# Turning q and k by transpositions of two row halves in place of quarter products, in an attention and bilinear FFN kernel

## The chip, the cores and the metric

The kernel runs on one core of a Trainium2 chip. The metric is the device time of one execution in microseconds (us). The core has five engines that run side by side, each through its own list of instructions in order: PE (TensorE, matmuls; its weight loads are shown apart as PEld), DVE (VectorE), ACT (ScalarE), POOL (GpSimd) and SP (SyncE). SP and ACT issue the DMA transfers here, and 16 DMA engines carry them out. A matmul takes its two operands from SBUF, the memory on the core, and writes to PSUM, a small memory[...] from which DVE and ACT take the results.

## The reference

```python
batch, n_heads, seq, head_dim = (8, 12, 448, 64)
n_tokens, d_model, d_ff = (3584, 768, 1536)

def rmsnorm(x, g):
    rms = np.sqrt(np.mean(x * x, axis=-1, keepdims=True) + 1e-06)
    return x / rms * g
q_n, k_n = (rmsnorm(q, g_q), rmsnorm(k, g_k))
scores = 1.0 / np.sqrt(q.shape[-1]) * np.matmul(q_n, k_n.transpose(0, 1, 3, 2))
scores = scores - np.max(scores, axis=-1, keepdims=True)
attn = np.exp(scores)
attn = attn / (np.sum(attn, axis=-1, keepdims=True) + 1e-09)
attn_out = np.matmul(attn, v)
x = attn_out.transpose(0, 2, 1, 3).reshape(B * S, H * D)
return (x @ w_a) * (x @ w_b) @ w_out
```

Inputs and output are fp32; the three weight matrices come in fp64. q and k are normalized per row of 64, attention runs over 448 positions in each of 96 heads, and its output goes through a bilinear feed-forward layer.

## The kernel before

**Attention** runs in 24 steps p, each of four heads of one batch: two pairs w = 0, 1 of two heads. For each p one tile each of q, k and v is loaded (function `loads`, line L424): pair w lies in partitions 64 w to 64 w + 63, its two heads h side by side, and each partition holds 7 consecutive positions j of 64 values. So a tile is [128, 2, 7 x 64], and a DMA moves runs of 7 x 64 values (1,792 bytes). Tiles of q and k have one buffer each, those of v two.

In `normalize`, ACT squares a tile (L459), DVE adds up the squares (L461) and scales them (L494), and POOL raises them to the power -0.5 (L496). DVE multiplies q by the result into the tile `qn` (`apply`, L500). k is not multiplied: its factor is applied later, as the scale of Exp.

A product of queries and keys needs both with head_dim on the partitions, so q and k are turned (`transposes`, and `turn_first` for p = 0). The turn is done on the PE by `quarter_turns` (L528): for each of the 7 positions j, 2 pairs w and 2 heads h a 64x64 block is multiplied with an identity, on one quarter of the PE's array. The result stands in a PSUM tile `pt` of two banks, one per pair, with head h in partitions 64 h to 64 h + 63. ACT copies it to `qkT` (L547 for k, L549 for q with the gains). The tile `pt` has the tag `sc`, of which there are two buffers, shared with the scores.

After that come, for each of the 7 blocks j of keys: `scores` (L587, four products on quarters of the array, tile `sc`), Exp of each head by ACT (L593, two of 448 columns), and `values` (L609, four products, accumulated in the tile `o`). The sums over the keys come from products with ones (L645) for p < 4, and for later p from additions by DVE and POOL (L623) and one such product. `invert`, `put_out` and `divide` do the division.

**The feed-forward layer** takes two batches at a time (beta = 0 to 3) and multiplies by a scheme with seven products in place of eight. Its first layer is `quarter_products` (L1294) for beta = 0 and 1 and `deep_products` (L871) for 2 and 3, its second `last_product` (L995) and `inner_products` (L1192). All of these are full-array products of 128x128. Before that, ACT and DVE round the fp64 weights to fp32 (`rounding`, L247 to L256) while attention runs.

**The order of the work** is not found on the chip. The kernel books 4,383 operations with `op(...)`, each with its engine, an expected duration, what it reads and writes and, on the PE, a mode ("quad" for quarters, "full"). `Plan.run` then issues them in a sequence that is written out in the source as the compressed string `ORDER`. Each engine's instructions follow in that sequence, and the semaphores between the engines follow from the tiles. The durations in the calls were for the making of the sequence and have no effect when the kernel runs; the same is so of the mode. In the sequence, feed-forward products of the two batches before stand among the attention of the next ones.

At the start the PE runs `warm` products (L409, identity by identity, 128x128) until q and k of p = 0 are there.

In the first part of the time, p = 0 to 11 lie within the first 220 us; p = 12 to 14 at 386 to 450; p = 15 at 536 and 686; p = 16 to 23 at 739 to 875. What follows is the feed-forward layer alone.

Of the kernel before, what the change touches and what calls it, by code (L numbers as in the profile page):

```python
# [20 lines left out]
def _float_of(bits):  # L21
# [11 lines left out]
    "c-rkZ2Xs}%wtHqyyXEwAOLEgg=m-g@5Aq_#hN2G<5JZZif$$(9KnP$U2@pU!5)cA01p)|sAPK!E7{Me)s#uT@ND+McY`n&=``iTZum4=@y|2Hy"  # L33
    "*mKXEGc&u--ZT3$;NDJ(B)<~~p~M5K=`sBlF%8QwJ&Mn75Tmn4(Xput{#M`vGPsvSx*;5#q2LIeGZ-8`-;DbupOp>M%x81qzU=!Z_j&ccrzW23"
    "o%!^H4F1FM<3<CpQPA)>j7%XT9!)003A|XHopU&6PIh+QKG^G>z8i|Iob^yx#;-1dRsS}rVDqGcjq3|GxK;rxgXP6gG@<BC@~=x_-0S0D<ziU4"
    "{AT{5?_klAuNM@3wE%usSayBE{8A_>D7kc%FaFFZeDhQ9mh)t_0c<0Da2C$2UwVqXUbdEOaFLR-l7Cr4ifjH-44sca^?|DI>foDi=Ix(nl3jam"
    "?A^s3-hJ&LckmKi^dEq{iv3XjF@fznpwd}+63WXfH^ZhaTjAJ&qwgHNCBUXX?5o-b^A5q@uMh0|66o3+aDDq4C@rsqedYV#-@E6+xo!1zjy)gl"
    "-u*%CnQc&W6pn8>+OVa%`t9nQf2=<Cef80AkG%8smbbsE+H$rU&RnZHbhzQ#p+oi1srLNlTItySqx(14?AvtYWbKh7M~=Q<Q(qHSf28hWT`hR4"
    "_gH(5Jw|HYQ9(I)u=*g}Jb2*1SKoXIJl%fd#*Wrdx$7_2ukPA)`R3)zyRLt8{mNILeOdY07nL_|^t^cS^U90zg)8b6$K?xRrEux|?<>!L`uV5-"
    "eC=w*l|NrSckS}!KV7+UIilj~Clw!8Uihfu{EqV#pMJXi%JvHnpR2fdQ9QrnA5WgEIPr1isk0w!ue^2ZM8oMn{rTh{w%<Ha(eQr5_h-Kge0#Ry"  # L40
    "Y~2~FzV7s?y1L5amrm4PxOm~z@$>K3Hq<t}_g=#XwYTa||GECX`ucO<D{=MTHhff9USD2U{YCld>t{bNFTeWsl@9@`o!d@B6&(8H5Y&8FbMQSl"
    "P+bevf2^v4jdh1>H^c8?KS1o>6R>CP?)R!b+g*8aUB%k-`?ssxw*hP``S_!XHL#7qX(u%7*?(&ftlkLgHk6gGU%zVWx~hYPhgQKBQea#Lcw_m6"
    "m6Yb^zX8ih{!;g8a{AN~fW?bo(ZU9}xo`n2m``BtTsS;8kJ8z&fIyzh1-X!$13B4{Jq@xkZ>GSc$uKE%3Z)qt851)o5E!>O9n!}Fq@_aY7}Equ"
    "NdXv1k_o`e!vS7;5ndby!-m4JAvp8G3or=gzc3I6z;kYQf9MN+pM_`p06fzhdXuN&siy!yc>*2>H$3_Xz{5SDM|bGn4Z0IE2>~E6DUm{FfL}cb"
    "F1WuFbm|C@5D)PkP;|R?0Bvb&)T(6*6c*PEn#DqF48%s`C^9lKB8rC7Fl7e>2>4y#^PUB-2f#AHGypUWKvxJMu3VBsa&t*;4#~;R70J|T(>^Mg"
    "YE6A(MoxCtG{_RN_{oze2?Q8G4uP?0S+8cLO-Y+FJ?*tzwq<rIOdcaLmILY2U}P%7*x9M6dG%?jspHa93Q{~PMvfdcYGewGn3J4L^I*)&Fltox"
    "@RXF{!$(XWo-%6kh?EJ*h59S$FTJ#amsNhKd+?BvjuFYj9E0HbLC?SV;-DczpMTzwJn*>z0|vSW3>`4Ak2`(9fd2gl_U|S1e^z+n8DV(O-aWbG"
    "XI~k@4etGd_>|yy`0<DPJ^q-Z$D_hCQV*e5k6zI2iJn~7BtGe(HNWou(9_+x#3#|Qi9Hh^c`Wha#2$&gdL(x1*`r(c?%iBnx+FdHxT|v#=X44a"
    "9i0VNCjo@`_zvwK?I=k-dI)X1wG{+LDaV>WNV)qdqaua&gfRQp5<A>ckf_}=8e(^N#DYD>ed3r#7?OlB8jA1lIm%f+i+Vkbr<y^Ty~a@lk(oSa"
    "w-~#Nj^;VPKa}J4dXa@`Qo~^O32!(2AcUhD$2b<wvC;rajEG>=@1@jY)Fg&MwY#{sT12(w1oiMUYU6=P3Frj0LD<=iLLYbr;}m!UM?G!aDC7&l"  # L50
    "MF7JjU>O8D8cH7mzflOdNYF;$h=#Zkl!n>(sD>@UN2wRZTS017Qwhk<TLjY$Nkk9?;Tt!6P2h_uaGhq1p`$0D2YyS>lhGqakN7Q1`JT`*<Ye;j"
    "FOyGQBQL#-3S5NxAxCS^4g2JsleC7>Ge;;_SM^R+)!WqrYwPG?I{4_<2Wkd$Uvf992kq&9Xb*R27q@Hg`Q1DF?b@-kA5_9Kr^-)OpP<M49NtIk"
    "f75$2J+^7nvF$*%l=u2-_n|}ouwiGf^_%we+I{J*b-gw~rSQah*jfgqXG+(Wo-Exh9zVWj{m#-gWu+x+N^6RXONwhY7H@^34eK`*?SE^-UMRb~"
    "yX?`OW##b5sxsJIu&H=spOuA$eF}HN>Ov?u_U`DS)msZ{3RbVKhQo)Kttwas-Ip(2R=O-df6dOK(vrf$!nOGu^9xs<E?!;s=BicsC8Y%=b?+9h"
    "Dk^w$>B_FKdIg?p%lGbuq-C&k>B7~O3o4c@TKVfYRxDb+Xny`ex^%<qOKHiH{KTd6<{ewSaOJAS3+Js^{>H)s%jPD|U(jXot_7WUyw-L8obq{d"
    "X3v|oY4)tQX63D)MZ3&Qnm(P)on5kE_N?5wujS?)nK^T2?vj~HXTH8@&#W0U9-Kj6%gvoVeO7MXrRlj{rsu9(H#0kX+JjSzvx|zdr?LmK9?Y4N"
    "4J12zDr7CqdOa&^e%8DPUY$rY=FHj(c?mNo&Bz>&2kF|0853awOu72nl=0&WCXS!karuO09rDx1rKe3!%bc8<nU*;*Eh8;+cEZG*jPa=%sjrTo"
    "Iwk$p^z_V~nVG4OHlchh)OAQ7dn|41eW{~IkA^9uMrEc<Ov%VdNg3a6!pL#y>21=-jvWhQ$0nyHk7+Y{%qzKVaz~HKgA~YXl`?YDh#9T&^0Km^"
    "<rEk)xaIg^T=vkhQ-?xa+?X*i8sZ>kL`+OS+V>?&BcdWG)<#bT!UO&K1^V_4*x?`I^Z6hNIG^Q#2f)Cy)HJ$ioi$KF*RZ1MAcLy3{*@b(LdUb9"
    "nIbvdnEbp0L=H0qgWf|_rFp=c-!WA6sNtHbs=DgaR1-hi8>*q{ieFI-MNvAas->7ZR%@zX^(&^Pw6k&THBB=*dKDAXNke3>VrZRo9TQUzlND?}"  # L60
    "T~^{%)uV*Vrly5xR;ZQW({wou=|WVb(pA}`D5$Wf6$&z}1j95m{E(5@E6cjtLDP`8tf@HEbWKk1$d;n38ZuE#S(S}=tRJ-iqWcYhN5hX(a=2{h"
    "x@`E25KWJ0uWP0eYG_`~w2&ALGXkot*!o+jnc6N4jZn~RMT^%BO*UmiR?!j}1r#N`soO3<MP-zWGitnQgv+uf%YIZYLDRfy1QLX!ma=ZBTAJBj"
    "vs6<LSK~ru%kSx6Aw3!t@|>as^>6Qy!(`1sa>Z0+*>fLSs-RmNt<~aDzN{-gT-5H@(Us^5v@TSZ1I<DVt%L6MYBp+!9ujIr#ap^J+|W(0ZiMQV"
    "H{OcWEkh6JvS!I43DG9{7I(>G?~-Dn!HU^d2}R?5%DZS4ZjDuqWq62fFB;KF_n--Aw;ZCN8&$>E0kJGpSCjo17E^G;g4Ts#tXQajJn?v>R}?N("
    "bUS?xhr{D=aHixY4zY!UxJ*&#>6WPIaEPMJ;+z9a!O2O2(p8WIL4HyYBquNPN;J`_lEj5LD04b3>T+<BqzHTq%9>F^qDfS=5J^ZB-f0oxB!u`w"
    "yM*|oqPhnB_lJZg_!-$2O51rn;T|s|9t)f4H$w@c`P=y;{H^_hpY!^(SkvPPL#0)sYnnyDtrH(+iq_nz>TNL!UCs#28Rjyn+X7zFCCMSlE?Fj`"
    "U`03umq0<_Ig#UecN?yah^ZuF0#PsofiMoW5^3;O!J93nE0rCL0p)uDCxTtB@OU*c#t3C`qC{g1kwo%*0^iIZNQ$u{!YLQvxCp|S8Ol6Hh++67"
    "W-^tvH<+x8n(TASZi}fd!4%sVZqX-+ZoK;)Oyw9a^1Q%{ju@uN9FyC*7?YV>ViIqEAdTc|CAplE$#8-<n9l4AT8ec@I&+Ik8<)#LWI?35&hyBN"
    "IyixgqfBBNM;UHJODCm*Q=*dSX96eiRN|;WWl5uI1l9>06PZhBj`u!Z&CHDj1K&yzC^F=621)U0E>WjwQ0f-jQqFBR(dFbFoXiO#dQ^;aa#Tm}"
    "7+7+Mbf+s0z3o6xQ{JW)*Kty?`d}QgccQVhxrlfQM{RMmmEaUCE(Z%C&DM-^ShqN1sROl8&>+z%Hh<Y|$CN7ZoSR4UILTI=j|?iWv=Af-T_P}r"  # L70
    "=WM-coC|FX%A;tl#8WYjLvwgWoj@d>cpYdi6EwTt(Fl&?IO1SL<cYz_|0GHx7biG4P2#Y35y{=0F(=dcV7;YMh4LRdV|nomZV+{&iyS0aLNPvq"
    "xQXO!ElIc|4nhP*%3T=#5+h8CV?5z0!*H~*UAU@aI$%JwcFIo9<>KVogjaYBFsJ?SM2hBAyVUASoMcQ;0Ean*tk6Zo)y&}>AS80=3(EE8I3hB%"
    "gD@BGjN~0rxcNlDMmZ!v&7929nh-IT#Kd4O60rqoLAYi#lqY@?8G(0@FU%Jm9TV{R0={;Bf7@{4ZAn_h+CyJxNQfug?+y4`hP7zv^Tq{2eV%A$"
    "SrJhdW@^{ahrA({-%nzQ5lbwO$BHll7N)Py^qS4Qa*Sq1StPod8SaZ#!wsVAG(sbIpqZvg67WQiG&Lhk4p+QB#bx<rx7)2_c*!nzdzahN+L$JW"
    "h&LK{F*efWjtY|lm`HxN<Wh;~6daP%3JDcx2v0E3+ek!`#OA8(h$9h>2pYu)Fs*pXxdf~YaqkpL1Jp?aj7k)1WgpK|V1~-cGWtEh5fAZ+R4^zq"
    "15g?8c8QCzi}{c7X7~8dg$B#=CLr*C3dql)82KCMf7<d7fWptk>2Kgk@4o5nKT`CL7(5K@QDYw**&PXXjc>5C(0<XT4$1!`#vPzR^ro)qMH?Bw"
    "9cE1ue!xCR+W1BPGt<8UK%21eA7LXd-0pARW=$;aeBHLqHkvkRd51}(B5+$fn@1D*9lR#5G&$|=CXw5NAa>If`{7oSzi&tX?!9O5{|@L+!nC89"
    "{xGKRqSD4i8bk=b8liD~mpC{TTxG%K#=&idO^CD+6Pg&@A%nX-o4DK-`2%r30&rKI+uFh%hPO3qvgfXG^hdlwf96mkKYw)o_)&c)Uw)h^x&8aA"
    "^S@Xi|LY9y!7l;mJs13VhLE2tr|u=&J@|zj67;__;r=UWL;mM(xqE4R4}K#2J5;O;O8"
# [68 lines left out]
def kernel(  # L148
# [126 lines left out]
    def fast_body(ld, wk, ps_s, ps_o, ps_mm, dram):  # L275
# [139 lines left out]
        def loads(p, nm):  # L415
# [4 lines left out]
            def emit():  # L420
                x = ld.tile([P, 2, NT * D], FP32, tag=nm, name=nm + "_sb", bufs=2 if nm == "v" else 1)
                for w in range(2):
                    pair = src[b, h0 + 2 * w:h0 + 2 * w + 2]
                    nc.sync.dma_start(x[low_high[w]], pair.rearrange("h (p j) d -> p h (j d)", j=NT))  # L424
                xs[nm, p] = x
            if p == 0 and nm != "v":
                def begin():
                    xs[nm, p] = ld.tile([P, 2, NT * D], FP32, tag=nm, name=nm + "_sb", bufs=1)

                def half(w):  # L430
                    pair = src[b, h0 + 2 * w:h0 + 2 * w + 2]
                    queue[("SP", "ACT")[w]].dma_start(
                        xs[nm, p][low_high[w]], pair.rearrange("h (p j) d -> p h (j d)", j=NT))
                op(None, 0.0, -11, begin, [], [f"{t}/{w}" for w in range(2)], new=[t])
                for w in range(2):
                    op(("SP", "ACT")[w], 0.7, -10, lambda w=w: half(w), [], [f"{t}/{w}"], kb=350)
                return
            op("SP", 1.28, p - (1.8 if nm == "v" else 2.0), emit, [f"firsts{PREP}"] if p >= HELD else [], [t], new=[t],
               kb={"q": 620, "k": 620, "v": 530}[nm], dmas=2)

        def loaded(p, nm):
            return [f"{nm}0/0", f"{nm}0/1"] if p == 0 else [f"{nm}{p}"]

        def normalize(p):
# [8 lines left out]
            def squares(s, nm):  # L453
                sq = tile_of(f"sq{nm}{p}", "sq", 1)

                def square():
                    x = xs[nm, p]
                    t = xs["sq", nm, p] = wk.tile([P, 2 * NT, D], FP32, tag="sq", name="sq")
                    nc.scalar.activation(t, x.rearrange("p h (j d) -> p (h j) d", d=D), AF.Square)  # L459
# [3 lines left out]
            def front(n):  # L463
# [10 lines left out]
                def times():  # L474
                    if n == 0:
                        qns[0] = wk.tile([P, 2, NT, D], FP32, tag="qn", name="qn")
                    nc.vector.tensor_tensor(
                        qns[0][:, :, j0:j1],
# [1094 lines left out]
```

## Time and profile before

| | |
|---|---|
| time, median of 3 runs | 1479.97 us (1479.83 to 1484.28) |
| time of the profiled execution | 1479.91 us |
| its span in the trace | 1478.1 us |
| PE busy | 1461.7 us, 99%, 10,238 matmuls |
| DVE, ACT, POOL busy | 986.4, 437.6, 328.9 us |
| DMA | 248.28 MB in 152,036 packets, mean 168 GB/s |
| granted PE clock | 0.999 |

A group line of the profile reads: source line, engine, operation, output<-input by tile names, tile of the array (for the PE), shape and count; then the sum of busy time and the mean ns of one; then the time that the engine stood idle before them and what ended it. A line of the timeline reads: start in us, length in us, engine, source line, operation, tiles, shape and count, and in brackets the idle time before. A matmul's length holds its way through the array, which overlaps with that of the next ones; what it occupies of the PE is the distance from its start to the next start. The first rows of the page divide the span into 40 equal slices and give busy tenths (9 is 90% or more). The chain of waits is followed back from the last instruction, at each step to what released it.

### The profile page before, as it was taken

To read this page: it belongs to the slowest core of one execution; us is meant where nothing else is said; L and a number is where in the kernel's file an instruction comes from. 1 tells how busy PE (TensorE), PEld (TensorE's weight loads), DVE (VectorE), ACT (ScalarE), POOL (GpSimd) and SP (SyncE) were. 2 spreads that over 40 slices of the span, in tenths; PEclk is the share of its full clock that TensorE was granted. 3 is DMA by queue.
4 is the path that set the end of the run, shared out by engine and by line. 5 is a ranking of instruction groups with operands and counts; after the bars stand their busy time and mean duration, and the time that the engine had idled before them with its cause. 6 is when DMAs were issued, how large, how long until landed. Compare 5 with 4: busy or idle time off the path is not lost.

```text
span 1478.1 us, 25741 instructions
## 1 busy us (share of the span) xinstructions
PE 1461.7 (99%) x10238; PEld 967.3 (65%) x10238; DVE 986.4 (67%) x1575; ACT 437.6 (30%) x792; POOL 328.9 (22%) x175
## 2 busy tenths in 40 slices
PE   9999999999999999999999999999999999999998
PEld 6444444555444555555454445799997899999898
DVE  6886799888665233344657766367687676767785
ACT  6787652112553000000257771011111011111100
POOL 3356632012242001110345540011110001121000
PEclk9999999999999999999999999999999999999999
DMA  8876456544533536446545535555465755555464
GB/s 256 247 210 176 123 165 219 197 163 157 158 116 120 159 128 205 154 150 188 180 139 141 156 84 172 174 166 159 146 186 178 248 170 158 159 164 156 149 211 131
DMA packets 152036, 248.28 MB, mean 168 GB/s; under 512 B 19556, under 2 KB 124516, under 8 KB 145252
## 3 DMA queue, kind: packets, MB, share of 16 engines
q1 hardware_dynamic: 123556, 192.61, 44.1%
q10 hardware_dynamic: 28352, 53.94, 10.8%
q8 instruction: 83, 1.36, 0.4%
q14 instruction: 45, 0.37, 0.1%
HBM read 188.35 MB, written 57.93 MB: 167 GB/s over the span
## 4 chain that ended last, share of the span: by engine, by line
PE 94%; DVE 2%; DMA 1%; ACT 1%; issue 1%; POOL 1%; SPq 0%; ACTq 0%; POOLq 0%; DVEq 0%
PE pq L1294 24%; PE dg L871 17%; PE po L995 17%; PE o L609 8%; PE sc L587 8%; PE da L871 6%; PE pt L528 3%; PE a L1192 2%; PE g L1192 2%; PE su L645 2%; PE e L1192 1%; PE b L1192 1%; PE d L1192 1%; PE warm L409 1%; ACT ET L593 1%
## 5 line engine op out<-in xcount | busy, mean ns | idle before, releaser
L1294 PE MATMUL pq<-x,st 128*128 128x448 f32 x1008 | 384.0, 541 | 0.6 <-ACT t L1319 0.5
L1294 PEld LDWEIGHTS pq<-x,st 128*128 128x128 f32 x1008 | 189.7, 190 | 190.2 <-issue 174.5
L593 ACT ACTIVATE ET<-sc,ms 128x448 f32<-128x448 f32 x336 | 190.8, 635 | 98.6 <-PE sc L587 65.1
L496 POOL TENSOR_TENSOR ms<-ms,expo 128x14 f32<-128x14 f32 x47 | 143.7, 3057 | 127.3 <-DVE ms L494 122.6
L871 PE MATMUL dg<-dT,st 128*128 128x224 f32 x672 | 167.5, 354 | 0.7 <-DVE dt L911 0.5
L995 PE MATMUL po<-st,hT 128*128 128x384 f32 x492 | 164.1, 488 | 0.0
L871 PE MATMUL dg<-x,st 128*128 128x224 f32 x672 | 163.1, 353 | 0.6 <-DVE dF L918 0.6
L587 PE MATMUL sc<-qkT 64*64 64x448 f32 x1344 | 153.0, 542 | 3.8 <-ACT ET L593 3.1
L609 PE MATMUL o<-ET,v_sb 64*64 64x448 f32 x1344 | 149.4, 538 | 0.0
L899 POOL TENSOR_TENSOR hT<-dF 128x448 f32<-128x448 f32 x42 | 48.1, 1163 | 422.3 <-DVE dF L894 418.4
L995 PEld LDWEIGHTS po<-st,hT 128*128 128x128 f32 x492 | 92.3, 190 | 65.5 <-issue 4.9
L871 PEld LDWEIGHTS dg<-dT,st 128*128 128x128 f32 x672 | 126.5, 190 | 2.9 <-DVE dt L911 1.1
L871 PEld LDWEIGHTS dg<-x,st 128*128 128x128 f32 x672 | 126.5, 190 | 2.9 <-DVE dF L918 2.2
L871 PE MATMUL da<-x,st 128*128 128x224 f32 x504 | 118.4, 352 | 0.0
L623 POOL TENSOR_TENSOR sum<-sum,ET 128x896 f32<-128x896 f32 x40 | 90.7, 2268 | 124.1 <-DVE sum L623 89.9
L587 PEld LDWEIGHTS sc<-qkT 64*64 64x64 f32 x1344 | 47.1, 132 | 81.1 <-issue 43.1
L871 PEld LDWEIGHTS da<-x,st 128*128 128x128 f32 x504 | 95.1, 190 | 0.3
L894 DVE TENSOR_TENSOR dF<-dF 128x896 f32<-128x896 f32 x84 | 92.6, 1104 | 3.5
L609 PEld LDWEIGHTS o<-ET,v_sb 64*64 64x64 f32 x1344 | 50.7, 133 | 65.4 <-issue 57.7
L884 ACT COPY dt<-da 128x224 f32<-128x224 f32 x84 | 28.8, 346 | 213.1 <-PE da L871 153.0
L623 DVE TENSOR_TENSOR sum<-sum,ET 128x896 f32<-128x896 f32 x60 | 65.0, 1084 | 37.3 <-POOL sum L623 20.6
L995 PE MATMUL po<-st,fin 128*128 128x384 f32 x252 | 86.4, 492 | 0.0
(147 smaller groups left out, 1677.6 us busy)
## 6 DMA issues: line engine op xcount, KB each, us to landing
st<-kept_o SPq DMA_DIRECT2D x28, 1152.0 KB
st<-kept_s SPq DMA_DIRECT2D x84, 320.0 KB
kept<-st ACTq DMA_DIRECT2D x12, 1344.0 KB
st<-kept SPq DMA_DIRECT2D x12, 1344.0 KB
st<-kept SPq DMA_DIRECT2D x84, 192.0 KB
ti<-kept_t SPq DMA_DIRECT2D x48, 288.0 KB
kept_s<-ds SPq DMA_DIRECT2D x30, 448.0 KB
v_sb<-in_v_dram SPq DMA_DIRECT2D x48, 224.0 KB
```

What stands on the lines that cost most here:

```text
L496: lambda: nc.gpsimd.tensor_tensor(msf(), msf(), expo[:, 0:2 * NT * (b - a)], ALU.pow), [], names)
L528: nc.tensor.matmul(t[low_high[h], w, (j - j0) * D:(j - j0 + 1) * D], lhsT=x[rows, h, j * D:(j + 1) * D], rhs=ident[rows, rows], start=True ...
L587: nc.tensor.matmul(t[low_high[w], e, 0:S], lhsT=qkTs[p][low_high[e], 1, w * S + j * D:w * S + (j + 1) * D], rhs=qkTs[p][low_high[e], 0, w ...
L593: nc.scalar.activation(E[:, e], scs[p, j][:, e, 0:S], AF.Exp, scale=rs[p][:, 1, e * NT + j:e * NT + j + 1])
L609: nc.tensor.matmul(os_[p][low_high[e], w, 0:S], lhsT=xs["v", p][low_high[w], e, j * D:(j + 1) * D], rhs=ETs[p, j][low_high[w], e], start=( ...
L623: two[e].tensor_tensor(sums[p], sums[p] if j > 1 else ETs[p, 0], ETs[p, j], ALU.add)
L871: nc.tensor.matmul(to(), lhsT=W(w), rhs=t(), start=not more and k == 0, stop=k == len(terms) - 1, skip_group_check=True)
L894: take("DVE", 1.09, lambda: V.tensor_tensor(F[to], F[to], F[other], ALU.add), allF(other), allF(to), lock=True)
L899: lambda: two[e].tensor_tensor(C(i, n), F[g][:, 0:S], F[g][:, S:2 * S], ALU.mult), allF(g),
L995: nc.tensor.matmul(held["po"][:, 0:HALF], lhsT=a[0]()[:, c], rhs=sts[beta, 12 + place_of[f]][:, c], start=(c == 0), stop=(c == MH - 1))
L1192: nc.tensor.matmul(held[bank], lhsT=x()[:, c], rhs=y(c), start=(start and c == 0), stop=(stop and c == MI - 1), skip_group_check=True)
L1294: nc.tensor.matmul(banks[bank][:, 0:S], lhsT=sts[at][:, f, c * P:(c + 1) * P], rhs=quads[x][:, c], start=(start and c == 0), stop=(stop an ...
```

## The change

k is loaded as [128, 7, 2, 64], with the two heads side by side within each position j, so the runs of its DMA are 64 values (256 bytes) long. `qn` gets the same layout: DVE's multiplication writes through a rearranged view. For each j and each pair w, one transposition then turns the [64, 128] block of both heads in one go; the pairs lie in the two row halves. There are 14 transpositions in a turn in place of 28 products. The copies by ACT and everything behind them see the same `pt` as before. The factors of k come out of the reduction in the order j, h, and Exp's scale is read there. Tiles of later stages that use k's buffer take its shape.

```diff
-                x = ld.tile([P, 2, NT * D], FP32, tag=nm, name=nm + "_sb", bufs=2 if nm == "v" else 1)
+                x = ld.tile([P, NT, 2, D] if nm == "k" else [P, 2, NT * D], FP32, tag=nm, name=nm + "_sb", bufs=2 if nm == "v" else 1)
...
-                    nc.sync.dma_start(x[low_high[w]], pair.rearrange("h (p j) d -> p h (j d)", j=NT))
+                    nc.sync.dma_start(x[low_high[w]], pair.rearrange("h (p j) d -> p j h d" if nm == "k" else
+                                                                     "h (p j) d -> p h (j d)", j=NT))
...
-            op("SP", 1.28, p - (1.8 if nm == "v" else 2.0), emit, [f"firsts{PREP}"] if p >= HELD else [], [t], new=[t],
-               kb={"q": 620, "k": 620, "v": 530}[nm], dmas=2)
+            op("SP", 1.28 if nm != "k" else 1.4, p - (1.8 if nm == "v" else 2.0), emit, [f"firsts{PREP}"] if p >= HELD else [], [t], new=[t],
+               kb={"q": 620, "k": 800, "v": 530}[nm], dmas=2)
...
-                    nc.scalar.activation(t, x.rearrange("p h (j d) -> p (h j) d", d=D), AF.Square)
+                    flat = (x.rearrange("p h (j d) -> p (h j) d", d=D) if nm == "q" else
+                            x.rearrange("p j h d -> p (j h) d"))
+                    nc.scalar.activation(t, flat, AF.Square)
...
-                qns[p] = wk.tile([P, 2, NT, D], FP32, tag="qn", name="qn")
+                qns[p] = wk.tile([P, NT, 2, D], FP32, tag="qn", name="qn")
                 nc.vector.tensor_tensor(
-                    qns[p],
+                    qns[p].rearrange("p j h d -> p h j d"),
...
-        def quarter_turns(t, x, j0, j1):
+        def turn_halves(t, x, j0, j1):

             for j in range(j0, j1):
                 for w in range(2):
                     rows = low_high[w]
-                    for h in range(2):
-                        nc.tensor.matmul(t[low_high[h], w, (j - j0) * D:(j - j0 + 1) * D], lhsT=x[rows, h, j * D:(j + 1) * D],
-                                         rhs=ident[rows, rows], start=True, stop=True)
+                    nc.tensor.transpose(t[:, w, (j - j0) * D:(j - j0 + 1) * D], x[rows, j].rearrange("p h d -> p (h d)"), ident[rows, rows])
...
-                op("PE", TURN, key, turn, [f"{nm}{p}" if n else f"qn{p}", f"half{p - 1}"], [pt], new=[pt], mode="quad")
+                op("PE", TURN, key, turn, [f"{nm}{p}" if n else f"qn{p}", f"half{p - 1}"], [pt], new=[pt], mode="half")
...
                     nc.scalar.activation(E[:, e], scs[p, j][:, e, 0:S], AF.Exp,
-                                         scale=rs[p][:, 1, e * NT + j:e * NT + j + 1])
+                                         scale=rs[p][:, 1, 2 * j + e:2 * j + e + 1])
```

The load of the first q and k and the first two turns (`half`, `front`, `turn_first`) change in the same way. The string `ORDER` is another one: the 4,383 operations are the same, with the same dependences, and their sequence is new throughout. Decoded against the list of operations, the PE's part of it (1,455 operations) sets the turns like this:

| | before | after |
|---|---|---|
| turns of k and q of one p side by side | 1 pair | 13 pairs |
| a turn with quarter products on both sides | 26 of 49 | 5 of 49 |
| a turn with full products on at least one side | 23 of 49 | 26 of 49 |
| changes between quarter, half and full tiles on the PE | 90 | 132 |

## The prediction, made before the changed kernel was run

> **What bounds the kernel now.** I read the slices and the chain of waits on the page first, then the groups of instructions by shape, then the PE's own timeline around single turns, and last the busy time by stretches.
>
> ```profile
> PE   9999999999999999999999999999999999999998
> ...
> DVE  6886799888665233344657766367687676767785
> ACT  6787652112553000000257771011111011111100
> ...
> DMA  8876456544533536446545535555465755555464
> ...
> PE 94%; DVE 2%; DMA 1%; ACT 1%; issue 1%; POOL 1%; SPq 0%; ACTq 0%; POOLq 0%; DVEq 0%
> ```
>
> The PE is full in every slice and is 94% of the chain that ended last. What the PE is spared is therefore spared in the whole time, as long as nothing else turns up late. The first five slices (each 37 us) have little spare time elsewhere: DVE and ACT at six to eight tenths, the DMA engines at up to eight.
>
> ```profile
> L528 PE MATMUL pt<-ident,qn 64*64 64x64 f32 x1344 | 25.3, 220 | 2.5 <-ACT rec L662 1.1 <-DVE qn L500 0.8 <-issue 0.6
> L528 PE MATMUL pt<-ident,k_sb 64*64 64x64 f32 x1344 | 25.0, 219 | 0.0
> L528 PEld LDWEIGHTS pt<-ident,k_sb 64*64 64x64 f32 x1344 | 23.9, 135 | 11.4 <-issue 5.3 <-ACT ET L593 4.8 <-DVE x L738 0.7
> ```
>
> These are the turns. There are 24 of k and 24 of q (that of the first q in two parts), each of 28 quarter products, and each product is two instructions (24 x 56 = 1344), since an fp32 matmul is run as two loads and two matmuls. The 220 ns of one are latency; the price of a turn has to be read from the timeline of the PE.
>
> ```profile
> 40.88 0.93 PE L609 MATMUL o<-ET,v_sb 64*64 64x448 f32 x8
> 41.63 0.99 PE L528 MATMUL pt<-ident,k_sb 64*64 64x64 f32 x56
> 42.44 1.69 PE L609 MATMUL o<-ET,v_sb 64*64 64x448 f32 x16
> 44.88 1.04 PE L528 MATMUL pt<-ident,qn 64*64 64x64 f32 x56 [0.75 <-DVE qn L500]
> 45.71 0.96 PE L645 MATMUL su<-ET,ones 64*64 64x448 f32 x8
> 46.61 0.98 PE L685 MATMUL inv<-rec,ones 1*64 1x448 f32 x8
> 47.52 0.98 PE L645 MATMUL su<-ET,ones 64*64 64x448 f32 x8
> ```
>
> From start to next start the turn at 41.63 holds the PE for 0.81 us (0.814 in single records, and so for every undisturbed turn between quarter products). Its 56 matmuls go four at a time, in 14 steps of 58 ns. Five lines down, `inv` with its one-row tiles stands between products of 64x64 tiles: they take 0.90 and 0.91 us where 0.75 is usual, so another tile shape costs about 0.15 us at each of its two ends.
>
> ```profile
> 739.10 1.04 PE L528 MATMUL pt<-ident,k_sb 64*64 64x64 f32 x56
> 740.08 4.14 PE L995 MATMUL po<-st,fin 128*128 128x384 f32 x12
> 744.14 1.04 PE L528 MATMUL pt<-ident,qn 64*64 64x64 f32 x56
> 745.01 1.69 PE L609 MATMUL o<-ET,v_sb 64*64 64x448 f32 x16
> ```
>
> A turn before full-array products takes 0.98 us (the first full matmul starts 148 ns after the turn's last, not 38), so leaving the tiles costs 0.11 us. Behind full products its first matmul comes 416 ns after the last full one where these follow one another by 323, and its own row is 51 ns longer: 0.144 us for going in. The mean is 0.127 us a switch.
>
> ```profile
> 0.00:50.00 50.00, 47.03 (x722) 27.28 (x726) 34.26 (x47) 34.22 (x52) 18.81 (x15) 1.00 0.81 243
> 50.00:100.00 50.00, 48.28 (x726) 23.51 (x721) 45.03 (x54) 41.10 (x66) 21.88 (x8) 1.00 0.87 260
> 100.00:150.00 50.00, 47.90 (x722) 19.92 (x717) 36.30 (x48) 38.16 (x65) 31.07 (x12) 1.00 0.57 161
> 500.00:600.00 100.00, 100.00 (x331) 52.67 (x330) 34.14 (x49) 5.06 (x9) 5.61 (x5) 1.00 0.53 166
> ```
>
> The columns are the stretch, its length, PE, PEld, DVE, ACT, POOL, clock, DMA share and GB/s. The PE idles some 7 us in the first 150 and hardly any later; from 50 to 100 us DVE is at 90%, ACT at 82%, DMA at 87%.
>
> **What the Trainium skill says.** "TensorEngine Tiling (Array Packing)", Key Properties: changing the tiling mode, not just the tile, drains the engine. The trace agrees, with the 0.11 to 0.15 us above. "TensorE: Matmul & The Clock Gate", Terms (xbus): weight loads and matmuls on trn2 have a transpose mode, "4× faster for FP32". The trace has no transposition, so this is open. The same page, LDWEIGHTS: a load takes its columns divided by 1.2 per ns, whatever its rows. The trace agrees for plain fp32 loads: 135 ns for 64 columns, 190 for 128, thus about 55 per 64. "DMA: Bandwidth & Descriptors", Specifications: runs under 512 B are below line rate. The trace has no runs of 256 B, but its mean packet times are 10 ns for 64 B, 29 for 512 and 113 for 1,792.
>
> **The change part by part.**
>
> *The turn itself.* 28 products become 14 transpositions of 64 rows by 128 columns, two at a time (one per row half): 7 steps. The step's price is not in the trace. At present a moving column takes 0.84 ns (448-column matmuls start 376 ns apart), twice the 1/2.4 ns of the same page's Back-to-back issue gap, so I count two passes in each instruction. Below: one pass for 64 columns is 27 ns, with the 3 ns a step has over 30, and 0.21 us a turn. Above: a 128-column load at the plain fp32 rate. The `warm` products, which load 128 columns for each matmul, start 112 ns apart: 7 x 112 = 0.78 us. If moreover each transposition is two instructions, or the two row halves don't overlap: 1.57 us. I take the mode as the page has it, fp32 in one pass: the load of 128 columns then takes what 64 take now in two, and paces the step at the same 58 ns: 7 x 58 = 0.41 us. The 46 turns after the first pair gain 46 x (0.814 - 0.41) = 18.6 us. The first pair's turns lie in the start, among `warm` products, and count as nothing; if they sit on that chain, they are worth half a microsecond.
>
> *Switches.* A transposition in fp32 uses tiles of 64x128, another shape than the 64x64 around it. With both order strings decoded against the list of operations, the PE's sequence has 90 changes of shape before and 132 after. That is 42 more, not 96 more, because the new order sets 13 of the pairs k, q side by side (one before) and many at the border of full products. 42 x 0.127 = 5.3 us lost. Bounds: nothing if going from 64x64 to 64x128 doesn't drain, 42 x 0.15 = 6.3.
>
> *The new order's waits.* A turn needs one of the two `sc` buffers, and a pair side by side needs both. The second turn then waits for the Exp of the latest scores (two of 635 ns), and behind it on the PE stand `o` and `su` products, then scores that wait for ACT's two copies (0.91 and 1.01 us). Before, the one such pair, at 134.5 us, had a second turn of 1.79 us, 0.98 over. Bounds: 0 to 13 x 0.98 = 12.7 us. In the new order most pairs have two quarter products (1.5 us) between the latest scores and the turns, which covers the two Exps; so I take 0.2 us a pair, 2.6 us.
>
> *k's load.* Runs become 256 B, 1,792 packets for 256. On a line between 64 and 512 B one takes 18 ns, so a pair's load holds the 16 engines 1792 x 18 / 16 = 2.0 us for 256 x 113 / 16 = 1.8. Bounds: at 10 ns 0.7 us less, at the 29 of 512 B 1.4 more. Some eight loads fall in the first 100 us: up to 11 us of DMA time, where 16 are free. The loads are issued about 11 us before their turn (30.22 for 41.63), which hides this; without that cover a turn would be late by up to 1.4 us. SP's issue (1.25 us for two) grows at most slightly, on a queue that has gaps. Nothing.
>
> *The rest.* Square, reduction, qn's multiplication and Exp's scale read or write the same elements in other places: 0.95, 1.08, 1.17 and 0.64 us as before, and DVE and ACT have the same work. Nothing.
>
> Sum: -18.6 + 5.3 + 2.6 = -10.7 us. The profiled execution took 1479.91 us (1478.1 of span and 1.8 around it), and the median is 1479.97: 1469.2.
>
> **Rivals.**
>
> *The load paces the step at the plain rate* (the slower side). Place: the 7 steps of every turn. If transpose mode shortens the matmul but not the load, a turn is 0.78 us, the gain is 46 x 0.03 = 1.4 us, and switches and waits stay: +6.5 us, 1486.4. It decides from 0.64 us a turn (92 ns a step) on. For it: loads in the trace follow the column count. Against it: the page names loads too.
>
> *Two instructions each, or halves one after the other*: 1.57 us a turn, +35 +8 = 1523. Against it: four tiles overlap now, and row halves are of the same sort.
>
> *One pass for the load as well as the move, hidden behind it*: 0.21 us, -27.8 + 7.9, 1460.
>
> *The gain is lost in the first 220 us.* Half of the turns lie there; at 50 to 100 us DVE, ACT and DMA have 10 to 18% left, and a PE that comes sooner waits for Exp. Then half stays: about 1475. Against it: rounding of weights, DVE's largest work there, is not what scores wait for.
>
> **How the numbers follow.** Forecast 0.42 (its own range 1464 to 1476: steps of 53 to 68 ns, waits of 0 to 5 us); lost in the first part 0.14; one pass throughout 0.08; load paces 0.28; doubled 0.08. About 0.3% (4.4 us) is what can be told from no change. Faster: 0.42 + 0.08 + half of 0.14 = 0.57. Same: the other 0.07 and 0.05 of the load's case (steps just over 92 ns) = 0.12. Slower: 0.23 + 0.08 = 0.31. The range 1461 to 1490 leaves out the doubled case and the end of the fastest.
>
> **What will show it.** A turn of about 0.41 us from start to next start less 0.13 for a switch; 336 matmuls each for k and q (14 x 24), not 672; PE gaps at pairs under 0.3 us; k's packets at about 18 ns, and no wait for k. Steps over 92 ns, PE waits for ACT that grow by more than 10 us, or PE idle time before 220 us that grows by the turns' gain, would prove me wrong.

## The result, and the profile after

| | before | after |
|---|---|---|
| median of nine runs each, side by side | 1479.38 us (1477.28 to 1484.28) | 1474.1 us (1471.52 to 1477.19) |
| ratio, 95% interval | | 0.9963 (0.995 to 0.9976) |
| profiled execution, its span | 1479.91, 1478.1 us | 1477.19, 1475.2 us |
| PE busy, matmuls | 1461.7 us, 10,238 | 1452.8 us, 8,222 |
| DMA | 248.28 MB, 152,036 packets | 248.02 MB, 188,884 packets |

The change saves 5.3 us (3.6 to 7.4 by the interval); 10.7 were predicted. The profiled execution of after is the slowest of its nine. A second profile of the same kernel, nearer the median (span 1471.4 us), is used below where the two differ. The lines of the turn are L530 in after (L528 before), and others move by one to three lines as well; in the kernels below whose sequence is cut together they are two lower than in after.

The slices and the chain on the page of after:

```profile
PE   7999999999999999999999999999999999999998
...
DVE  4998699888675233344668776466677676666785
ACT  5887752111554000000257770011111011111100
...
DMA  8876467554442555556555635555554755555355
...
PE 87%; DVE 5%; DMA 3%; ACT 2%; issue 1%; SPq 0%; POOL 0%; ACTq 0%; DVEq 0%
```

The PE is still full from the second slice on, but its share of the chain has fallen from 94% to 87%: the end now hangs on DVE, DMA and ACT in 10% of the span, where it was 4%. DVE is busy for 998.3 us, 986.4 before. The first slice, 9 before, is 7.

The groups of the turns, by shape:

```profile
L530 PE MATMUL pt<-ident,qn 64*128 64x64 f32 x336 | 15.9, 232 | 1.1 <-DVE qn L503 0.8 <-ACT ET L594 0.2
L530 PE MATMUL pt<-ident,k_sb 64*128 64x64 f32 x336 | 15.5, 229 | 5.0 <-ACT ET L594 3.8 <-DMA k_sb<-in_k_dram 1.2
L530 PEld LDWEIGHTS pt<-ident,k_sb 64*128 64x128 f32 x336 | 12.3, 138 | 19.8 <-ACT ET L594 9.6 <-issue 6.1 <-ACT sq L462 1.4
```

There are 336 where 1,344 stood: one instruction for a transposition (24 x 14), in place of two for each of four quarter products. A load now takes 128 columns, and lasts 138 ns where one of 64 columns lasted 135.

The timeline of the PE in after, around the turns that were shown of before (a pair side by side, and the turns at 740 us):

```profile
47.68 0.93 PE L610 MATMUL o<-ET,v_sb 64*64 64x448 f32 x8
48.55 0.65 PE L530 MATMUL pt<-ident,k_sb 64*128 64x64 f32 x14
49.52 0.65 PE L530 MATMUL pt<-ident,qn 64*128 64x64 f32 x14 [0.32 <-DVE qn L503]
50.10 0.98 PE L646 MATMUL su<-ET,ones 64*64 64x448 f32 x8
...
739.97 0.65 PE L530 MATMUL pt<-ident,k_sb 64*128 64x64 f32 x14
740.55 4.14 PE L996 MATMUL po<-st,fin 128*128 128x384 f32 x12
744.62 0.65 PE L530 MATMUL pt<-ident,qn 64*128 64x64 f32 x14
745.19 1.73 PE L610 MATMUL o<-ET,v_sb 64*64 64x448 f32 x16
```

From its start to the next start a turn takes 0.58 us (739.97 to 740.55), 0.98 before at the same place. The transpositions start 29 ns apart, and 14 of them make 0.41 us; the rest is the change of shape. With quarter products on both sides one adds 0.11 us ahead (`o` at 47.68 would be over after 0.75, at 48.43; the turn starts at 48.55), and 0.17 us in and behind the turn. A turn that stands alone there so costs 0.69 us in all, where it was 0.81: its two changes of shape, 0.14 us each, take back most of the 0.41 us that it saves.

The busy time by stretches:

```profile
0.00:50.00 50.00, 42.14 (x422) 25.40 (x422) 29.57 (x40) 31.01 (x48) 17.86 (x14) 0.97 0.87 228
50.00:100.00 50.00, 49.59 (x546) 19.32 (x546) 47.12 (x58) 41.66 (x64) 21.48 (x7) 1.00 0.89 259
100.00:150.00 50.00, 48.05 (x498) 17.37 (x490) 41.17 (x48) 40.11 (x70) 35.09 (x13) 1.00 0.60 160
500.00:600.00 100.00, 99.87 (x290) 52.58 (x289) 34.44 (x49) 6.02 (x10) 5.66 (x5) 1.00 0.54 163
```

The PE idles 7.9 us in the first 50, where it was 3.0. Most of that is one place, which the second profile of this kernel doesn't have:

```profile
14.44 1.74 SPq L424 DMA_DIRECT2D k_sb<-in_k_dram  x2
16.81 4.51 SPq L424 DMA_DIRECT2D v_sb<-in_v_dram  x2
...
29.37 0.95 ACT L462 ACTIVATE sq<-k_sb 128x896 f32<-128x896 f32 x1 [5.02 <-DMA k_sb<-in_k_dram]
...
31.42 0.65 PE L530 MATMUL pt<-ident,k_sb 64*128 64x64 f32 x14 [3.78 <-ACT ET L594]
```

k of p = 1 is issued at 14.4 us and is there only at 29.4, so its turn comes 3.8 us late. The line names Exp as the releaser, because its semaphore came last; on ACT that Exp stands behind the square of the same k, which waits 5.02 us for the DMA. The new sequence sets the load of v right behind k, at 16.8 us (28.2 before). In the second profile the PE is busy for 46.83 us of these 50.

### The profile page after: what moved, and what is told of

Read it like the earlier page. It is cut to its first block, busy times and chain, and to the rows that moved or that the text cites. A ratio compares the mean times of both kernels' runs of the same rounds, so it can differ in the third digit from the quotient of the medians.

```text
span 1475.2 us, 21710 instructions
## 1 busy us (share of the span) xinstructions
PE 1452.8 (98%) x8222; PEld 944.5 (64%) x8222; DVE 998.3 (68%) x1575; ACT 438.1 (30%) x792; POOL 332.6 (23%) x175
## 2 busy tenths in 40 slices
DMA packets 188884, 248.02 MB, mean 168 GB/s; under 512 B 62564, under 2 KB 161380, under 8 KB 182116
## 4 chain that ended last, share of the span: by engine, by line
PE 87%; DVE 5%; DMA 3%; ACT 2%; issue 1%; SPq 0%; POOL 0%; ACTq 0%; DVEq 0%
PE pq L1295 24%; PE dg L872 17%; PE po L996 17%; PE sc L588 6%; PE o L610 6%; PE da L872 6%; PE a L1193 2%; PE g L1193 2%; DMA k_sb<-in_k_dram 1%; PE su L646 1%; PE pt L530 1%; PE b L1193 1%; PE e L1193 1%; PE d L1193 1%; DMA q_sb<-in_q_dram 1%
## 5 line engine op out<-in xcount | busy, mean ns | idle before, releaser
L1343 POOL TENSOR_TENSOR hT<-hT,t 128x448 f32<-128x448 f32 x12 | 16.6, 1382 | 292.8 <-DVE t L1341 265.5
```

## The experiments

Theories for the 5.4 us that are missing: the new sequence costs more in waits than the 2.6 us of the prediction; k's load in short runs costs something after all, in the start above all (K); a switch costs more than 0.127 us. Another comes from the profile of after: the load of v, issued early, delays that of k (V). In all kernels but `quad_new_order` and `quad_k_interleaved` the turns are those of the change, but for the first two of k in `first2_by_head`.

**The change in the old sequence.** The string of the sequence is that of before, all else is the changed kernel:

```diff
 ORDER = (
-    "c-rkZ33OFOmba>2z4y1bzrW_^X9WZi2#d0afb@VOwk)Hl;0^%=5+ETV3JD;KU}OzzfUt>S6SF|r6PB<f5kWR-MYcw9qaDHNwx@ee-<JfTTYE-5"
+    "c-rkZ2Xs}%wtHqyyXEwAOLEgg=m-g@5Aq_#hN2G<5JZZif$$(9KnP$U2@pU!5)cA01p)|sAPK!E7{Me)s#uT@ND+McY`n&=``iTZum4=@y|2Hy"
...
```

> The change without its new sequence: k interleaved and turns as transpositions, in the sequence of the kernel before. By count this sequence has 157 changes of tile shape (90 before, 132 in the changed kernel) and one pair of turns side by side. If the loss against the forecast comes from waits of turns set side by side (theory O), it is gone here: -18.6 us for the turns, +67 x 0.127 = 8.5 for switches, so about -10 us, ratio 0.993. If it comes from k's load in runs of 256 bytes (theory K, 4 to 5 us), about -5.5 us, ratio 0.996.

**The new sequence with the old turns.** The changed kernel with the functions of before (load, square, `qn`, scale of Exp too):

```diff
-                    nc.tensor.transpose(t[:, w, (j - j0) * D:(j - j0 + 1) * D], x[rows, j].rearrange("p h d -> p (h d)"), ident[rows, rows])
+                    for h in range(2):
+                        nc.tensor.matmul(t[low_high[h], w, (j - j0) * D:(j - j0 + 1) * D], lhsT=x[rows, h, j * D:(j + 1) * D],
+                                         rhs=ident[rows, rows], start=True, stop=True)
...
```

> The new sequence alone: quarter products and k's load as before. 92 changes of tile shape, so nothing from switches. Theory O: the waits of the 13 pairs side by side show, +2.6 us as forecast (ratio 1.002), or up to +8 (1.005) if they are the whole of what is missing. Theory K: the sequence costs no more than about 1 us, ratio 1.000 to 1.001.

**The load of k alone.** Before's sequence and quarter turns, with q and k laid out as in the change:

```diff
-                        nc.tensor.matmul(t[low_high[h], w, (j - j0) * D:(j - j0 + 1) * D], lhsT=x[rows, h, j * D:(j + 1) * D],
+                        nc.tensor.matmul(t[low_high[h], w, (j - j0) * D:(j - j0 + 1) * D], lhsT=x[rows, j, h],
                                          rhs=ident[rows, rows], start=True, stop=True)
...
```

> k's load in runs of 256 bytes alone: quarter products and sequence as before, the blocks read from the interleaved tile. Theory K: +4 to +5 us, ratio 1.003, and in the trace ACT's square of k waits for its DMA within the first 50 us. Theory O and the forecast: nothing, ratio 1.000.

**The first two k by head.** The changed kernel, but k of p = 0 and 1 is loaded in runs of 1,792 bytes and turned by quarter products:

```diff
+        BY_HEAD = 2
...
-                x = ld.tile([P, NT, 2, D] if nm == "k" else [P, 2, NT * D], FP32, tag=nm, name=nm + "_sb", bufs=2 if nm == "v" else 1)
+                x = ld.tile([P, NT, 2, D] if nm == "k" and p >= BY_HEAD else [P, 2, NT * D], FP32, tag=nm, name=nm + "_sb", bufs=2 if nm == "v" else 1)
...
```

> The changed kernel with k of the first two steps loaded by head in runs of 1,792 bytes and turned by quarter products, which costs the PE two turns x 0.3 us. Theory K, if the first loads are what is late: 4 to 5 us below the changed kernel, ratio to before 0.993. If late loads of all steps count alike, or theory O holds: as the changed kernel, 0.996.

These four ran together on one chip, beside 26 runs of before with a median of 1478.21 us. The groups below ran on other chips, so kernels of different groups are compared by what they gain against before in their own group:

| | median (range) | ratio to before | by the ratio |
|---|---|---|---|
| change in the old sequence | 1470.27 (1469.45 to 1470.76) | 0.9948 (0.9935 to 0.9962) | -7.7 us |
| new sequence, old turns | 1484.51 (1482.05 to 1486.71) | 1.0048 (1.0034 to 1.0062) | +7.1 us |
| load of k alone | 1479.8 (1478.27 to 1482.87) | 1.001 (1.0003 to 1.0016) | +1.5 us |
| first two k by head | 1473.41 (1472.25 to 1475.64) | 0.9968 (0.9956 to 0.998) | -4.7 us |

The turns and the load without the new sequence gain more than the whole change (7.7 us, for 5.5 by the ratio), and the new sequence by itself costs 6.3 us as a difference of the medians, 7.1 by the ratio. The 25 changes of shape that it spares are worth about 3.5 us: the gain that is missing went into the sequence. The load of k costs 1.5 us, a small part. Taking it away at the two places where it stood in the way in the profile of after gives nothing that could be told (0.9968 for 0.9963). The two quarter turns take about 0.6 us back, so up to a microsecond may hide there, but not four, and K falls as the main cause.

The trace of the new sequence with the old turns shows only a part of its cost. It is of the second fastest of its five executions (1482.19 us), and before was traced in another group (1479.91). Between the two traces the span grows by 2.2 us, and the sum of the PE's waits from 9.4 to 10.4 us. So about four of the 6.3 us are in no trace that was kept.

What the load alone does is seen in the waits of the PE in `quad_k_interleaved` (L531 is the turn there; the columns are the total in us, the times, the longest):

```profile
PE pt L531 <- DMA k_sb<-in_k_dram: 1.7, 3, 0.9
```

Before has no wait for k at all. Packets of 256 bytes take a mean of 24.0 ns in this kernel (a median of 18; a mean of 22.7 in after), against 113.0 for the 1,792 bytes of before, so the load of k for one p (1,792 packets, both pairs) holds the 16 engines for 1792 x 24.0 / 16 = 2.7 us, not 1.8.

**Where in the sequence.** Next the sequences were joined. `new_then_old` follows the new one for about 240 us and the old one from there on, `old_then_new` the other way about; `v1_later` is the changed kernel with one operation moved, the load of v of p = 1 to behind that of q of p = 2; `after_again` is the changed kernel itself. In all of them only the string differs, as in the first diff, and with it the order of every engine's work; in `v1_later` its first line is now

```diff
-    "c-rkZ33OFOmba>2z4y1bzrW_^X9WZi2#d0afb@VOwk)Hl;0^%=5+ETV3JD;KU}OzzfUt>S6SF|r6PB<f5kWR-MYcw9qaDHNwx@ee-<JfTTYE-5"
+    "c-rkZ33OFOmba>2z4y1bzrW_^X9WZi2#d0a0qFrnY*|K8!5sn$BtQZoND_7gBWqX_2%8u-F$;t}VF^nT5o8k;*&4--b_A!jr+ZG{p9G;>dqz3qoSq)5e"
...
```

> The changed kernel once more, unaltered, beside the three that follow on one chip, so that differences of 2 to 4 us between them can be told. Both theories: ratio to before 0.996, and in its trace v of the second step issued right behind k of it, near 16 us.

> The changed kernel with one operation moved: the load of v of the second step is issued after q's of the third, as in the kernel before (near 28 us), not right behind k's of the second (near 16 us). Theory V (this load crowds k's 1,792 small packets in the fullest stretch of the DMA engines): the PE's wait for the second k, 3.8 us in the profile of the changed kernel, goes; 2.5 to 4 us less than the changed kernel, ratio to before 0.994. Theory O (the loss lies all over the sequence): as the changed kernel, 0.996.

> The changed kernel; the operations of about the first 240 us in the new sequence, all later ones in the sequence of before; 143 changes of tile shape. If the new sequence loses in its first part (theory V, or waits among the first steps): as the changed kernel, 0.996. If it loses later: as transpositions in the old sequence, 0.995 or below.

> The other way about: the first 240 us in the sequence of before, the rest in the new one; 146 changes of tile shape. If the loss lies in the first part: as transpositions in the old sequence or 1 us better (11 switches fewer), ratio 0.994. If it lies later: 0.996.

Beside 32 runs of before with a median of 1478.67 us:

| | median (range) | ratio to before |
|---|---|---|
| changed kernel again | 1473.32 (1471.64 to 1476.83) | 0.9965 (0.9952 to 0.9978) |
| v of p = 1 later | 1474.29 (1472.2 to 1477.34) | 0.9966 (0.9953 to 0.9979) |
| new, old from 240 us on | 1473.97 (1471.88 to 1478.57) | 0.9967 (0.9958 to 0.9975) |
| old, new from 240 us on | 1470.64 (1470.26 to 1472.82) | 0.9946 (0.9928 to 0.9963) |

The early load of v makes no difference, and V falls. With the old sequence in the first 240 us and the new one behind, the gain is that of the old one throughout (0.9946 and 0.9948), with the new one in front it is that of the changed kernel (0.9967 and 0.9965): what is lost on balance stands in the first 240 us. Against the old sequence throughout (7.9 us below before by the medians) the new one in front spares 14 changes of shape (143 for 157), about 2 us, and gains 3.2 us less; behind 240 us it spares 11, about 1.5 us, and gains nothing by them (8.0 us). By this estimate it loses about 5 us in front and 1.5 behind, together what `quad_new_order` lost.

**Before or behind 155 us.** The same with the seam at about 155 us; the string is again all that differs:

```diff
-    "c-rkZ33OFOmba>2z4y1bzrW_^X9WZi2#d0afb@VOwk)Hl;0^%=5+ETV3JD;KU}OzzfUt>S6SF|r6PB<f5kWR-MYcw9qaDHNwx@ee-<JfTTYE-5"
+    "c-rkZ33yh;wP)t8|8n>HZ~2oy8)2s;!3|PmQ7eiT5fDTHK?9+X1qgu{NCE_uRU~W)AtcC-KoSB0*%Ams2*?hiA}F9}6>XufmiPL;p8F>OU%&cZYkiv^G"
...
```

> The changed kernel with the new sequence for the first 155 us (the turns of p = 0 to about 8) and the old sequence from there on; nothing of the computation is left out. The loss of the new sequence is known to lie in its first 240 us (1474.0 against 1470.3 for the old sequence throughout). Theory S (it lies in the start, where the v loads come earlier, the first pairs stand side by side and DVE is 90% full): about 1473.5 us, ratio 0.9965. Rival F (it lies from 155 to 240 us, in full products that wait for DVE's reading of hT, U and t and scores that wait for rec): about 1470.8 us, ratio 0.9947. Between them, near 1472, if it is spread over both.

> The changed kernel with the old sequence for the first 155 us and the new sequence from there on; nothing of the computation is left out. Theory S (the loss lies in the start): about 1470.5 us, ratio 0.9945. Rival F (it lies from 155 to 240 us): about 1473.5 us, ratio 0.9965. Near 1472 if it is spread over both.

New to 155 us and old from there on: 1471.48 us (1469.43 to 1472.62), ratio 0.9945 (0.9926 to 0.9965). Old to 155 us and new from there on: 1478.1 us (1474.36 to 1481.75), ratio 0.9997 (0.9989 to 1.0005). The second is slower than either sequence by itself, which no theory had; its timeline of the PE shows why:

```profile
154.06 2.52 PE L1293 MATMUL pq<-x,st 128*128 128x448 f32 x6
158.52 0.24 PE L528 MATMUL pt<-ident,k_sb 64*128 64x64 f32 x1 [1.94 <-DMA k_sb<-in_k_dram]
159.64 1.00 PE L528 MATMUL pt<-ident,k_sb 64*128 64x64 f32 x13 [0.87 <-DMA k_sb<-in_k_dram]
160.57 3.57 PE L1293 MATMUL pq<-x,st 128*128 128x448 f32 x6
164.07 1.73 PE L586 MATMUL sc<-qkT 64*64 64x448 f32 x16
```

At the seam SP issues v (152.69 us) and then k (154.15), only 4.4 us before the turn; in the changed kernel k's load is issued at 149.70, 7.4 us before its turn, and in the old sequence 9.9. The turn waits 2.8 us in its two halves, and the full products behind it take 3.50 us from start to next start, where six take 2.45 elsewhere. So 3.9 us of this kernel's time, in the profiled execution, belong to the seam. That is what a load of k costs where its cover, the time between its issue and its turn, is gone; whether runs of 1,792 bytes would have been there in time was not run.

Before has a median of 1478.01 us in this group. Without the seam's 3.9 us the second kernel would be 3.8 us below it; with the new sequence in front of 240 us it was 4.7, with the old one 8.0. The first kernel is 6.5 us below before by the medians, about halfway between these two, and 8.1 by its ratio (0.9945), level with the old sequence. So S (all in the start) falls, and F (from 155 to 240 us) holds for between half of the loss and the whole of it; the intervals of 0.9945 and 0.9967 still touch, so the share is rough. What stands there is seen when the PE's timelines of two kernels with the same turns are laid side by side. First the changed kernel (second profile):

```profile
182.47 2.52 PE L1295 MATMUL pq<-x,st 128*128 128x448 f32 x6 [0.46 <-DVE hT L1348]
...
196.65 0.65 PE L530 MATMUL pt<-ident,k_sb 64*128 64x64 f32 x14
198.10 2.52 PE L1295 MATMUL pq<-x,st 128*128 128x448 f32 x6 [0.80 <-DVE hT L1348]
...
203.56 0.98 PE L588 MATMUL sc<-qkT 64*64 64x448 f32 x8 [0.53 <-ACT ET L594]
...
207.68 0.65 PE L530 MATMUL pt<-ident,qn 64*128 64x64 f32 x14
209.38 0.98 PE L588 MATMUL sc<-qkT 64*64 64x448 f32 x8 [1.05 <-ACT rec L663]
210.29 2.52 PE L1295 MATMUL pq<-x,st 128*128 128x448 f32 x6
213.37 2.52 PE L1295 MATMUL pq<-x,st 128*128 128x448 f32 x6 [0.55 <-DVE t L1336]
```

Then the change in the old sequence, same stretch:

```profile
200.11 0.65 PE L530 MATMUL pt<-ident,k_sb 64*128 64x64 f32 x14
200.69 0.98 PE L588 MATMUL sc<-qkT 64*64 64x448 f32 x8
201.60 2.52 PE L1295 MATMUL pq<-x,st 128*128 128x448 f32 x6
...
208.17 0.98 PE L646 MATMUL su<-sum,ones 64*64 64x448 f32 x8
210.24 0.65 PE L530 MATMUL pt<-ident,qn 64*128 64x64 f32 x14 [1.09 <-ACT rec L663]
210.97 2.52 PE L1295 MATMUL pq<-x,st 128*128 128x448 f32 x6
```

With its line of 0.31 us at 219.56, the new sequence waits 3.70 us here, in six places. The old one waits 1.09, and then 0.38 and 0.49 behind 217 us: 1.96. None of the new sequence's waits is at a pair side by side. They are full products that come before DVE has emptied PSUM (`hT`, `t`), and scores that come before ACT has read (`ET`, `rec`). The new sequence with the old turns has the same six waits, at the same operations (0.45, 0.28, 0.53, 0.56, 0.55 and 0.30, 2.67 in all), where before has 1.09 us.

The PE's own list need not be the reason. Ahead of the first wait one group of scores stands between the two full products in both sequences (178.69 to 182.47, and 178.53 to 181.79). What differs is when DVE comes to the reading. The new sequence (second profile):

```profile
178.01 2.86 POOL L624 TENSOR_TENSOR sum<-sum,ET 128x896 f32<-128x896 f32 x1 [0.63 <-DVE sum L624]
178.85 3.04 DVE L739 TENSOR_TENSOR x<-x,rec 128x448 f32<-128x448 f32 x2
181.81 0.61 DVE L1348 TENSOR_TENSOR hT<-U,pq 128x448 f32<-128x448 f32 x1
```

The old one:

```profile
179.58 0.61 DVE L1348 TENSOR_TENSOR hT<-U,pq 128x448 f32<-128x448 f32 x1
180.11 0.61 DVE L739 TENSOR_TENSOR x<-x,rec 128x448 f32<-128x448 f32 x1
```

The new sequence sets two divisions `x` ahead of `hT`, and the first of them, which runs beside an addition `sum` on POOL, takes 2.51 us of the 3.04, where 0.61 is usual. The same comes at 205.59 (2.21 us beside a `sum`): ACT's copies `rec` wait 1.00 us for it, and the scores at 209.38 wait for ACT. These two chains are 1.5 of the 3.7 us. With the old turns both slow divisions are there too (2.50 and 2.51 us). At 198.10 and 213.37 too DVE has other work ahead of the reading: a reduction `ms`, which stands behind `hT` in the old sequence, and three steps of rounding. No run changes DVE's part of the sequence alone, so what this is worth in the whole time was not measured.

In front of 155 us only one wait was traced: in the changed kernel the second turn of the pair at 44 us waits 1.03 us in the second profile, and 1.64 to 1.97 in `new_to_155`, `v1_later` and `new_then_old`. In these three it waits for its `qn`, which stands on DVE behind a reciprocal that itself waits 1.69 to 2.04 us for a DMA. There is a wait of 1.46 us in the old sequence at 40.9 us too (scores for Exp), which the new one doesn't have. Which places make up the rest stays open.

## Why the prediction came out half right

Its sum was -18.6 + 5.3 + 2.6 + 0 = -10.7. The terms by the runs, each in its kernel:

| term | predicted | measured | by |
|---|---|---|---|
| turns | -18.6 | -18.7 | 46 turns at 0.814 less 0.407 us (single records of before and after) |
| switches, 42 | +5.3 | +5.9 | 0.14 each, from the turns that stand alone in after |
| new order's waits | +2.6 | +6.3 | new sequence with the old turns: 1484.51 for 1478.21 |
| k's load | 0 | +1.6 | load alone: 1479.8 for 1478.21 |
| sum | -10.7 | -4.9 | measured as a whole: -5.3 |

**The turn was right.** It was taken at 0.41 us in 7 steps of 58 ns, each instruction single, and it is that: two transpositions, one per row half, go in 58 ns. The Trainium skill's page named in the prediction, "TensorE: Matmul & The Clock Gate", Terms, says "4× faster for FP32" of the transpose mode; what this turn shows is a factor of two (0.407 us for 0.814) against quarter products, which already ran four at a time.

**The switches were nearly right**: 0.14 us each for 0.127. In the old sequence the same change brings 67 more of them (157 for 90), because there a turn mostly stands by itself between other shapes. That kernel is the check of the terms: 18.7 for the turns less 67 x 0.14 = 9.4 less 1.6 for the load make 7.7 us, and 7.9 were measured (5.6 to 9.6 by the interval of the ratio). Setting turns in pairs saves 25 switches, worth 3.5 us, and that is all that is known to be gained by the new sequence.

**The step that failed is "The new order's waits".** It said: "so I take 0.2 us a pair, 2.6 us". Waits were looked for at the pairs only. The turns' own waits were 2.5 us before; they come to 1.0 us in the second profile of after and to 6.0 in the first, 5.0 of it for k. What the step left out is that a sequence made anew moves the other 1,400 operations of the PE as well, and those of DVE, ACT, POOL and SP. Measured by itself it costs 6.3 us (5.0 to 9.2 by the interval of the ratio), 3.7 more than the term, and the joined kernels put most of it within the first 240 us. What the traces show of it is 1.6 to 1.7 us of waits more from 155 to 240 us, none at a pair: full products and scores whose buffers are read later than before, at four of the six places because of what stands ahead of the reading on DVE's list. For the rest no wait was found, and its cause stays open. The counts of shapes and of products around the turns, on which the term was based, say nothing of that.

*The rest* was put at nothing because DVE has the same work. It has, but not the same time: DVE is busy 12 us longer in after, and 11 us longer with the new sequence and the old turns (997.0 us).

**k's load was put at nothing, and costs 1.6 us.** A packet was taken at 18 ns from a line between 64 and 512 bytes: that is the median, but the mean is 22.7 to 24.0. The cover was 9 us or more in the old sequence for every load but the first; the new one leaves 7.4 us at two places. Where it was 4.4, at the seam, the turn waited 2.8 us, twice the 1.4 that was stated. For the first k there is no cover from the start: its turn waits 1.06 us for the DMA in the change in the old sequence, nothing before. The prediction had left the first pair out as "nothing".

**The rivals.** The load at the plain rate, the doubled case and the single pass are all excluded by the step of 58 ns. "The gain is lost in the first 220 us" had the time nearly right (about 1475), and the place, but not the reason: in the old sequence, with half of the turns in the same 220 us and the same engines beside them, the gain comes out as the sum has it (7.9 us for 7.7), and scores wait 2.9 us for Exp where they waited 3.1 before. A PE that comes sooner at its turns does not lose it again at Exp; with the other sequence it does lose.

Of the signs named, 336 matmuls each and the turn of 0.41 us came true, the gaps at pairs under 0.3 us only in most places (0.32 in the lines above, 1.03 in the second profile), 18 ns for k's packets as a median only, "no wait for k" did not. No disproof named came about: the steps are 58 ns, the waits for ACT did not grow by 10 us, and the PE's idle time before 220 us grew from 7.9 us to 13.6 in the first profile and 9.7 in the second, by less than the turns' gain there (22 turns, 9 us).

The change in the old sequence, at 1470.27 us (7.7 us under before by its ratio), and the old sequence with the new one from 240 us on, at 1470.64 (8.0 us), are both faster than the changed kernel by their medians; the intervals of the ratios overlap.

## What to carry to other kernels

When one change brings a cheaper operation and a new sequence, price the sequence as a change of its own: for each buffer, ask how much work stands between the product that fills it and the next that needs it, and what stands ahead of the reading on the list of the engine that empties it, not only what stands around the operation that was changed. The quickest test of such a pair is to run each half alone, and then to join the two sequences at a chosen time and see on which side of it the loss stays. A seam makes waits of its own, so its timeline is to be read before its time is believed.

## What was not expected of the hardware

- An fp32 transposition of 64 rows by 128 columns is one load and one matmul; two on different row halves overlap, 29 ns apart in the mean. Its load of 128 columns lasts 138 ns, where the plain fp32 load of 64 columns lasted 135.
- A short stop of the PE can cost more than its length. After the waits at the seam, the granted clock fell; these are the stretches of 5 us of that kernel (the clock is the third number from the end):

```profile
150.00:155.00 5.00, 5.00 (x32) 1.96 (x31) 3.55 (x7) 3.54 (x6) 4.49 (x2) 1.00 0.16 42
155.00:160.00 5.00, 2.19 (x12) 0.99 (x12) 2.46 (x4) 1.38 (x4) 3.48 (x2) 0.93 0.86 144
160.00:165.00 5.00, 5.00 (x30) 2.49 (x31) 2.98 (x5) 2.61 (x4) 2.07 (x1) 0.73 0.87 174
165.00:170.00 5.00, 5.00 (x42) 1.90 (x36) 1.44 (x2) 3.17 (x6) 1.82 (x2) 1.00 0.57 106
```

With 2.8 us of waiting came a clock of 0.73 in the stretch behind it, and six full products that took 1.05 us longer than elsewhere. In the first profile of after, the stop of 3.8 us at 31 us goes with a clock of 0.97 over the first 50. In windows of 3 us the clock is 0.50 there: from 159.5 us here, from 32.5 in that profile, and from 45.5 in `v1_later`, behind a stop of 1.8 us; each time the trace has it at half for 3.4 us. In `new_then_old` a stop of 2.0 us at 43 us was followed by none.
- DVE's multiplications `x` and `qn` are slow beside POOL's additions `sum`. In the second profile the six that start during one take 2.2 to 3.0 us (three of each), where by themselves `x` takes 0.61 and `qn` 1.07; beside POOL's power `ms`, eight `x` keep 0.61 to 0.64. Each of the six ends after POOL's addition does, `x` by 0.5 us and `qn` by 1.0. In the old sequence three operations are slow beside POOL (1.9 to 2.5 us).
- Kernels that begin with the new sequence scatter more: 5.7 us between the fastest and slowest of nine runs of after, 1.3 us over five runs of the change in the old sequence. Part of it goes with the clock: the five runs of after at a clock of 0.999 took 1471.5 to 1474.9 us, the four at 0.998 took 1474.1 to 1477.2. That the short cover of the loads of k is the reason was not tested.
